# Two more pairs of blocks in layer one, with sums of weights made earlier and reloaded

## The chip, the cores and the metric

The kernel runs on one core of a Trainium2 chip. The metric is the device time of one execution in microseconds; lower is better. TensorE's matmul side is called PE and its weight loads PEld; DVE is VectorE, ACT is ScalarE, POOL is GpSimd and SP the sync engine, whose queue issues most DMAs.

## What is computed

A long convolution by FFT over 2 x 3008 tokens of 256 channels, and behind it two feed-forward layers of 256 to 2048 to 256. The weights come as 64-bit floats.

```python
X = np.fft.rfft(x, axis=1)
y = np.fft.irfft(X * F, n=x.shape[1], axis=1).astype(np.float32)   # F: filt_r + 1j * filt_i
x = y.reshape(6016, 256)
h = x @ moe_w_in                                  # layer one
g = np.where(h > 0.0, h, np.exp(np.minimum(h, 0.0)) - 1.0)
x = (g @ moe_w_out).astype(np.float32)
h = x @ moe2_w_in                                 # layer two
g = h * np.clip(h + 3.0, 0.0, 6.0) / 6.0
out = (g @ moe2_w_out).astype(np.float32)
```

## The kernel before

**Numbers and tiles.** Every operand of a matmul is held as a high part and a low part (fp32r), and a product is three matmuls (`mm3`, lines 83 to 86). The 6016 tokens are 12 blocks, ten of 512 columns and two (5 and 11) of 448. The 2048 hidden channels are 16 chunks f of 128. A first-layer product of one block and one f has two halves c, a second-layer product two halves d.

**Single blocks.** Layer one starts with blocks 0 to 2 side by side and goes on with the blocks of `SINGLES` one by one. A unit is one block and one f: 6 matmuls into the hidden channel (`g1`), ELU (ACT twice at lines 422 and 423, DVE at line 424), a split into high and low (`g_split`, ACT line 80 and DVE line 81), and 6 matmuls of the second product (`g2`), three units later. `NU` is the number of units, 160 here. The list `pre` holds what is issued ahead of each unit, its slot; a pair group has four slots.

**Pairs.** The other blocks are worked in pairs by Winograd's form of Strassen's scheme: a group is one pair and two f (q = 0 to 7), with seven block products (`prod`) where eight would be needed, and eight second products (`second`). The seven products need sums of the data blocks (`x_sums`, `x_part`, 4 and 7 operations for a pair) and sums of the weights (`w_sums`, three sums for two f). In the group, key (k, d) names one of four hidden tiles. `add` (line 543) joins two banks on DVE; for layer one and the keys (0, 0) and (0, 1) a min follows on DVE (line 546) and ACT does one exponential (line 559); the keys (1, 0) and (1, 1) take a Relu and an exponential on ACT (lines 556 and 557). `gate` (line 566 for layer one) and `low` (line 579) are DVE's, `high` (line 574) is ACT's. PE's order in a group of layer one is: products 1 and 2, second (0, 0) of the group before, products 6 and 5, second (1, 1), product 7, second (1, 0), half of second (0, 1), product 4, the other half, product 3 (`elu_group`). DVE's order from the end of a group is: `add` (0, 1) and its min, then in the next group `low` (1, 1), `add` (0, 0) with its min, `gate` (0, 1), `low` (1, 0), the first slot's jobs, `gate` (0, 0), `low` (0, 1), on which half of second (0, 1) waits.

**Filling.** Weights of layer two are taken apart from their 64-bit words on DVE and ACT while the units run (`w_words`, `w_parts`, and `w_sums`), and stored to DRAM (`scrw`, `scrs`), to be loaded from GpSimd's queue when layer one has released its tiles (`w_load`, `s_load`). `filling` lists these steps, 176 of them, and `count` says how many are issued in each slot. Layer one's own sums of weights are in there as well: chunks 0 to 2 early, in the tile that the FFT's `zt` had, chunks 3 to 7 at the very end of the filling, in tiles of the pool `p4` (21 tiles) that live until the pair round is over. The second batch's FFT runs in slots 48 to 96 beside the units: its filter products are DVE's lines 192 and 193, GpSimd's line 195, and splits on ACT and DVE (line 81) or GpSimd.

**Layer two** is six pairs, in the same form, with another gate.

Of the kernel before, what the change touches and what calls it, by code (L numbers as in the profile page):

```python
# [30 lines left out]
SINGLES = [3, 4, 5, 6, 11, 7, 8]  # L31
PAIRS = [[(9, 10)], [(0, 1), (2, 3), (4, 6), (7, 8), (9, 10), (5, 11)]]
# [15 lines left out]
def fft_conv_moe_moe2(ctx, tc, xp, fq, sg, cs1, cs1t, cs2, ci2, ci1, ident, w1i, w1o, w2i, w2o, out):  # L48
# [249 lines left out]

    def s_tile(layer, q):
        if q >= 3:  # L300
            sums[layer, q] = t4([P, 2, 4, P], F32R)
            return
        if q == 0:
            sums[layer] = p12.tile([P, 3, 2, 4, P], F32R, tag="zt", name=name("zt"))
        sums[layer, q] = sums[layer][:, q]

    def w_sums(layer, q):
# [24 lines left out]
        if layer:  # L332
            nc.sync.dma_start(scrs[q], _f32(r.rearrange("p q i f -> p (q i f)")))
        yield

# [129 lines left out]
    def x_sums(l, p, i):  # L465
# [7 lines left out]
        eng = nc.vector if (l, p) in ROUNDS[:2] else nc.gpsimd  # L473
# [55 lines left out]
    class Group:  # L529
# [10 lines left out]
        def add(self, key, u, bank_):  # L540
# [3 lines left out]
            if not self.l and key[0] == 0:  # L544
# [3 lines left out]
        def relu(self, key):  # L548
# [6 lines left out]
            elif key[0] == 1:  # L555
# [233 lines left out]
    def filling():  # L789
        yield from sums_run(range(3))  # L790
        yield from conv2
        yield from sums_run(range(3, GROUPS))
# [4 lines left out]
    count = {52: 2, 53: 1, 54: 2, 55: 1, 56: 2, 57: 1, 58: 1, 59: 2}  # L797
    count.update({85: 2, 86: 4, 87: 2, 88: 1, 89: 2, 90: 1, 91: 5, 92: 3, 93: 3})
    count.update({NU + n: 1 for n in range(5, 17, 2)})
    left = n_fill - sum(count.values())  # L800
    other = {n: 1 for n in (94, 95, 99, 108, 109, 115, 124, 125, 131, 140, 141, 147, 158)}
    other.update({n: other.get(n, 0) + 1 for n in (134, 138, 139, 142, 143, 146, 147, 150, 154, 155)})
    room = {n: 7 if 112 <= n < 128 else 8 for n in range(94, NU)}
    total, had, jobs = sum(room.values()), 0, left + sum(other.values())
    for n in range(94, NU):
        had += room[n]
        want = -(-jobs * had // total) - sum(other.get(m, 0) for m in range(94, n + 1))
        count[n] = max(0, want - sum(count[m] for m in range(94, n)))
    assert sum(count.values()) == n_fill
    for n, k in sorted(count.items()):  # L810
        at(pre, n, steps, fill, k)
    for q in range(GROUPS):
        at(pre, NU + max(4 * q + 5, 14), s_load, q)
    for f in range(NF):
        at(pre, NU + 4 * (f // 2) + 8, w_load, f)
# [5 lines left out]
    }  # L821
    for i, (l, p) in enumerate(ROUNDS):
        for q, jobs in AHEAD.items():
            for j, (fn, arg) in enumerate(jobs):
                lag = 2 + j if i == 0 else 0 if i == 1 and fn is x_part else 2
                at(pre, NU + 4 * (GROUPS * (i - 1) + q) + lag, fn, l, p, arg)
# [253 lines left out]
```

## Time and profile before

| | |
|---|---|
| median of 3 runs | 1105.84 us (1105.46 to 1106.04) |
| profiled execution, its own time | 1105.2 us |
| its span, first to last instruction | 1103.4 us |
| matmuls (PE) | 5046 |
| busy share PE, PEld, DVE, ACT, POOL | 99%, 83%, 84%, 73%, 11% |
| granted clock of TensorE | full speed (1.0) |

The page gives busy time by engine and for 40 slices of the span; a timeline lists instructions by start; windows give each engine's busy time in a stretch; waits say which instruction waited for which. In this execution unit 48 is at about 196 us and unit 94 at 357 us, the pair round of layer one (blocks 9 and 10) runs from about 532 to 614 us, and layer two from there on.

### The profile page before, as it was taken

What the parts mean: (1) busy time and instruction counts of PE and PEld (TensorE: products, weight loads), DVE (VectorE), ACT (ScalarE), POOL (GpSimd) and SP (SyncE); (2) the same over time, 40 slices, a digit from 0 to 9 for tenths busy, and PEclk for the clock granted to TensorE, in tenths of its full rate; (3) what the DMA queues carried; (4) which work ended last, traced back from release to release, by engine and by line L of the source; (5) the groups of instructions that cost most, each with busy time, mean ns of one, the idle gap of its engine ahead of it and who ended that gap; (6) DMA issues with size and microseconds to landing.
All of it is one profiled execution on the core that took longest, in us unless ns stands there. A gap on an engine that the chain in (4) does not pass through costs nothing.

```text
span 1103.4 us, 14295 instructions
## 1 busy us (share of the span) xinstructions
PE 1095.1 (99%) x5046; PEld 912.8 (83%) x5046; DVE 925.7 (84%) x1495; ACT 801.2 (73%) x1426; POOL 116.9 (11%) x109
## 2 busy tenths in 40 slices
PE   9999999999999999999999999999999999999998
PEld 6688888788799889888888888888888888888997
DVE  5889998789988999999898877778777787777766
ACT  3587777887677787887788777667667767766665
POOL 4500000035520000000011110010010010000000
PEclk9999999999999999999999999999999999999999
DMA  9991100455544434323155400100100100100100
GB/s 298 292 315 56 29 1 1 142 179 180 167 120 144 148 117 154 112 77 134 39 172 176 168 20 20 39 20 20 39 20 20 39 18 17 39 1 1 39 1 34
DMA packets 55784, 99.44 MB, mean 90 GB/s; under 512 B 4768, under 2 KB 33440, under 8 KB 55712
## 3 DMA queue, kind: packets, MB, share of 16 engines
q1 hardware_dynamic: 51424, 85.59, 23.6%
q0 software_dynamic: 3456, 12.58, 3.6%
q8 instruction: 39, 0.64, 0.2%
q10 hardware_dynamic: 832, 0.36, 0.1%
q14 instruction: 33, 0.27, 0.1%
HBM read 64.18 MB, written 34.34 MB: 89 GB/s over the span
## 4 chain that ended last, share of the span: by engine, by line
PE 90%; DVE 4%; DMA 2%; issue 1%; ACT 1%; POOL 1%; SPq 0%; POOLq 0%; ACTq 0%; DVEq 0%
PE ps L84 29%; PE ps L85 28%; PE ps L86 28%; PE ps L219 1%; PE ps L139 1%; DMA scr<-t 1%; DVE t L81 1%; DMA t<-in_xp 1%; POOL t L195 1%; DMA t<-scr 1%; PE ps L183 1%; PE ps L152 0%; PE ps L200 0%; DVE t L192 0%; PE ps L892 0%
## 5 line engine op out<-in xcount | busy, mean ns | idle before, releaser
L84 PE MATMUL ps<-t,w 128*128 128x512 f32 (+1 forms) x1256 | 486.7, 387 | 1.5 <-DVE t L81 1.1
L85 PE MATMUL ps<-t,w 128*128 128x512 f32 (+1 forms) x1256 | 484.2, 386 | 0.0
L86 PE MATMUL ps<-t,w 128*128 128x512 f32 (+1 forms) x1256 | 484.2, 385 | 0.0
L84 PEld LDWEIGHTS ps<-t,w 128*128 128x128 f32 x1256 | 236.1, 188 | 48.9 <-DVE t L579 1.5
L86 PEld LDWEIGHTS ps<-t,w 128*128 128x128 f32 x1256 | 235.9, 188 | 44.1
L85 PEld LDWEIGHTS ps<-t,w 128*128 128x128 f32 x1256 | 236.1, 188 | 42.9
L81 DVE TENSOR_TENSOR t<-t,t 128x512 fp32r<-128x512 f32 (+2 forms) x257 | 190.3, 748 | 3.0 <-ACT t L80 1.7
L80 ACT ACTIVATE t<-t 128x512 fp32r<-128x512 f32 (+2 forms) x269 | 160.4, 610 | 21.3 <-POOL t L195 17.8
L579 DVE TENSOR_TENSOR t<-t,t 128x512 fp32r<-128x512 f32 (+1 forms) x224 | 154.1, 706 | 22.2 <-ACT t L574 20.9
L537 ACT ACTIVATE t<-ps 128x512 f32<-128x512 f32 (+1 forms) x168 | 99.0, 589 | 87.1 <-PE ps L86 85.9
L422 ACT ACTIVATE t<-ps 128x512 f32<-128x512 f32 (+1 forms) x160 | 93.3, 583 | 69.8 <-PE ps L86 69.2
L574 ACT ACTIVATE t<-t 128x512 fp32r<-128x512 f32 (+1 forms) x224 | 134.3, 617 | 4.9 <-DVE t L564 4.7
L543 DVE TENSOR_TENSOR t<-ps,t 128x512 f32<-128x512 f32 (+1 forms) x168 | 113.3, 677 | 26.3 <-ACT t L537 21.6
L424 DVE SCALAR_TENSOR_TENSOR t<-t,ps 128x512 f32<-128x512 f32 (+1 forms) x160 | 107.0, 669 | 28.8 <-ACT t L423 25.9
L564 DVE SCALAR_TENSOR_TENSOR t<-t,t 128x512 f32<-128x512 f32 (+1 forms) x144 | 98.7, 712 | 33.7 <-ACT t L554 33.4
L554 ACT ACTIVATE t<-t,three 128x512 f32<-128x512 f32 (+1 forms) x144 | 97.4, 709 | 35.4 <-DVE t L543 34.7
L423 ACT ACTIVATE t<-t 128x512 f32<-128x512 f32 (+1 forms) x160 | 99.5, 622 | 5.1
L564 DVE SCALAR_TENSOR_TENSOR t<-t,ps 128x512 f32<-128x512 f32 (+1 forms) x48 | 32.6, 678 | 29.0 <-ACT t L554 29.0
L86 PE MATMUL ps<-t,t 128*128 128x512 f32 (+1 forms) x140 | 54.1, 386 | 0.0
L84 PE MATMUL ps<-t,t 128*128 128x512 f32 (+1 forms) x140 | 54.0, 386 | 0.0
L85 PE MATMUL ps<-t,t 128*128 128x512 f32 (+1 forms) x140 | 54.0, 386 | 0.0
L554 ACT ACTIVATE t<-ps,three 128x512 f32<-128x512 f32 (+1 forms) x48 | 32.6, 680 | 28.9 <-PE ps L86 28.9
(99 smaller groups left out, 998.5 us busy)
## 6 DMA issues: line engine op xcount, KB each, us to landing
t<-in_fq SPq DMA_DIRECT2D x24, 512.0 KB, 6.4
scrw<-t SPq DMA_DIRECT2D x16, 512.0 KB, 2.8
w<-scrw POOLq DMA_DIRECT2D x16, 512.0 KB, 4.0
t<-in_xp SPq DMA_DIRECT2D x16, 384.0 KB, 6.0
scr<-t SPq DMA_DIRECT2D x24, 256.0 KB, 2.8
t<-scr SPq DMA_DIRECT2D x16, 384.0 KB, 4.9
scrx<-t SPq DMA_DIRECT2D x10, 512.0 KB, 3.3
t<-scrx SPq DMA_DIRECT2D x10, 512.0 KB, 3.4
```

Of the source, the lines that this page charges most:

```text
L80: nc.scalar.activation(hi, src, AF.Copy)
L81: eng.tensor_tensor(out=lo, in0=src, in1=_f32(hi), op=ALU.subtract)
L84: nc.tensor.matmul(acc, wh, xl, start=start, stop=False, skip_group_check=more)
L85: nc.tensor.matmul(acc, wl, xh, start=False, stop=False, skip_group_check=more)
L86: nc.tensor.matmul(acc, wh, xh, start=False, stop=stop, skip_group_check=more)
L423: nc.scalar.activation(r[:, :n], r[:, :n], AF.Exp, scale=-1.0)
L424: nc.vector.scalar_tensor_tensor(out=r[:, :n], in0=r[:, :n], scalar=-1.0, in1=acc[:, :n], op0=ALU.add, op1=ALU.max)
L543: nc.vector.tensor_tensor(out=self.h[key][:, :n], in0=bank_[:, :n], in1=u[:, :n], op=ALU.add)
L554: nc.scalar.activation(r[:, :n], h, AF.Relu, bias=three)
L564: stt(out=r, in0=r, scalar=6.0, in1=h, op0=ALU.min, op1=ALU.mult)
L574: nc.scalar.activation(gh[:, : self.n], g[:, : self.n], AF.Copy)
L579: nc.vector.tensor_tensor(out=gl[:, :n], in0=g[:, :n], in1=_f32(gh[:, :n]), op=ALU.subtract)
```

## The change

Blocks 7 and 8 leave the singles and become a second pair of layer one, ahead of 9 and 10. `NU` is 128 then, the two pair rounds of layer one take 64 slots, and layer two begins at slot `L2` = 192 as before. Eight groups of 45 matmuls take the place of 32 units of 12.

All of layer one's sums of weights are made first in the filling (26 steps in slots 45 to 61, 6 in 85 and 86), then the weights of layer two, which now run on through both pair rounds and 14 slots of layer two. The sums 3 to 7 are stored to DRAM (`scr0`) and loaded again in each pair round, one group ahead of their use, from GpSimd's queue. The loads of layer two's sums from chunk 3 on, and of its last two weight chunks, come later. In a group of layer one only key (0, 1) keeps its min on DVE; (0, 0) takes the Relu on ACT. The operand sums of the first round of layer two are DVE's (`ROUNDS[:3]`). `LATER` says where the operands of the next pair are made during a pair round of layer one.

```diff
-SINGLES = [3, 4, 5, 6, 11, 7, 8]
-PAIRS = [[(9, 10)], [(0, 1), (2, 3), (4, 6), (7, 8), (9, 10), (5, 11)]]
+SINGLES = [3, 4, 5, 6, 11]
+PAIRS = [[(7, 8), (9, 10)], [(0, 1), (2, 3), (4, 6), (7, 8), (9, 10), (5, 11)]]
...
+    scr0 = {q: dram.tile([P, 1024], F32, name=f"scr0_{q}") for q in range(3, NF // 2)}
...
-        if layer:
-            nc.sync.dma_start(scrs[q], _f32(r.rearrange("p q i f -> p (q i f)")))
+        if layer or q >= 3:
+            nc.sync.dma_start(scrs[q] if layer else scr0[q], _f32(r.rearrange("p q i f -> p (q i f)")))
...
+    def s0_load(q):
+        s_tile(0, q)
+        nc.gpsimd.dma_start(sums[0, q].rearrange("p q i f -> p (q i f)"), scr0[q])
...
-        eng = nc.vector if (l, p) in ROUNDS[:2] else nc.gpsimd
+        eng = nc.vector if (l, p) in ROUNDS[:3] else nc.gpsimd
...
-            if not self.l and key[0] == 0:
+            if not self.l and key == (0, 1):
                 self.g[key] = t2([P, 512])
                 nc.vector.tensor_scalar_min(self.g[key][:, :n], self.h[key][:, :n], 0.0)
...
-            elif key[0] == 1:
+            elif key != (0, 1):
                 nc.scalar.activation(r[:, :n], h, AF.Relu, scale=-1.0)
                 nc.scalar.activation(r[:, :n], r[:, :n], AF.Exp, scale=-1.0)
...
-        yield from sums_run(range(3))
+        yield from sums_run(range(GROUPS))
         yield from conv2
-        yield from sums_run(range(3, GROUPS))
+        yield from sums_run([])
...
-    count = {52: 2, 53: 1, 54: 2, 55: 1, 56: 2, 57: 1, 58: 1, 59: 2}
+    count = {n: 1 for n in range(45, 52)}
+    count.update({n: 2 for n in range(52, 62)})
+    count[58] = 1
+    L2 = NU + 4 * GROUPS * len(PAIRS[0])
...
-    count.update({NU + n: 1 for n in range(5, 17, 2)})
...
-        want = -(-jobs * had // total) - sum(other.get(m, 0) for m in range(94, n + 1))
+        want = -(-236 * had // 800) - sum(other.get(m, 0) for m in range(94, n + 1))
         count[n] = max(0, want - sum(count[m] for m in range(94, n)))
+    left, late = n_fill - sum(count.values()), L2 + 14 - NU
+    for n in range(late):
+        count[NU + n] = left * (n + 1) // late - left * n // late
...
-        at(pre, NU + max(4 * q + 5, 14), s_load, q)
+        at(pre, L2 - 4 * GROUPS + 14 if q < 3 else L2 + 4 * q - 4, s_load, q)
+        if q >= 3:
+            for r in range(len(PAIRS[0])):
+                at(pre, NU + 4 * (GROUPS * r + q - 1), s0_load, q)
     for f in range(NF):
-        at(pre, NU + 4 * (f // 2) + 8, w_load, f)
+        at(pre, max(L2 - 4 * GROUPS + 4 * (f // 2) + 8, L2 + 16 if f > 13 else 0), w_load, f)
...
+    LATER = {
+        2: [(x2_load, 0, 2), (x2_load, 1, 2)], 3: [(x_sums, 0, 2)], 4: [(x_sums, 1, 2), (x_part, 1, 0)],
+        5: [(x_sums, 2, 2), (x_part, 2, 0)], 6: [(x_sums, 3, 2), (x_part, 6, 0)],
+        7: [(x_part, 5, 0), (x_part, 7, 0)], 8: [(x_part, 4, 0), (x_part, 3, 1)],
+    }
```

## Rows read from the trace of the kernel before

**Rows 1.** the first part of the page: busy time, share of the span, instructions:

```profile
PE 1095.1 (99%) x5046; PEld 912.8 (83%) x5046; DVE 925.7 (84%) x1495; ACT 801.2 (73%) x1426; POOL 116.9 (11%) x109
```

**Rows 2.** timeline of PE in layer two: start, duration (us), engine, line, instruction:

```profile
749.94 0.39 PE L84 MATMUL ps<-t,w 128*128 128x512 f32 x1
...
759.46 0.39 PE L84 MATMUL ps<-t,w 128*128 128x512 f32 x1
```

**Rows 3.** windows: length; busy time of PE, PEld, DVE, ACT, POOL:

```profile
480.00:490.00 10.00, 10.00 (x46) 8.27 (x45) 9.93 (x19) 7.61 (x15) 0.00 (x0) 1.00 0.13 52
...
570.00:580.00 10.00, 10.00 (x46) 8.26 (x45) 9.77 (x17) 8.31 (x15) 1.42 (x3) 1.00 0.51 157
```

**Rows 4.** timeline of DVE among the single blocks:

```profile
481.00 1.28 DVE L81 TENSOR_TENSOR t<-t,t 128x512 fp32r<-128x512 f32 x2
...
482.21 0.68 DVE L284 TENSOR_TENSOR t<-t,t 128x512 f32<-128x512 f32 x1
...
487.33 0.75 DVE L323 TENSOR_TENSOR t<-t,t 128x256 f32<-128x256 f32 x2
```

**Rows 5.** timeline of DVE in the pair round, groups 2 and 3:

```profile
552.74 0.68 DVE L543 TENSOR_TENSOR t<-ps,t 128x512 f32<-128x512 f32 x1
...
557.87 0.68 DVE L579 TENSOR_TENSOR t<-t,t 128x512 fp32r<-128x512 f32 x1
...
562.92 0.69 DVE L543 TENSOR_TENSOR t<-ps,t 128x512 f32<-128x512 f32 x1
...
563.64 0.43 DVE L546 TENSOR_SCALAR t<-t 128x512 f32<-128x512 f32 x1
...
563.99 0.68 DVE L579 TENSOR_TENSOR t<-t,t 128x512 fp32r<-128x512 f32 x1
```

**Rows 6.** timeline of PE in group 2 of the pair round:

```profile
550.77 0.39 PE L84 MATMUL ps<-t,w 128*128 128x512 f32 x1
...
558.60 0.50 PE L84 MATMUL ps<-t,w 128*128 128x512 f32 x1
...
558.94 0.39 PE L85 MATMUL ps<-t,w 128*128 128x512 f32 x1
```

**Rows 7.** waits from 520 to 640 us: total, number, longest:

```profile
DVE t L566 <- ACT t L557: 6.6, 14, 0.9
...
PEld ps L84 <- DVE t L579: 1.1, 3, 0.6
...
PEld ps L84 <- ACT t L537: 0.5, 2, 0.4
```

**Rows 8.** timeline of DVE in slots 59 and 60, with idle time before:

```profile
233.93 1.42 DVE L329 TENSOR_TENSOR t<-t,zt 128x512 f32<-128x512 f32 x1 [0.27 <-ACT zt L327]
...
239.29 0.69 DVE L424 SCALAR_TENSOR_TENSOR t<-t,ps 128x512 f32<-128x512 f32 x1 [0.69 <-ACT t L423]
```

**Rows 9.** timeline of POOL (GpSimd): its additions of line 195:

```profile
277.27 1.28 POOL L195 TENSOR_TENSOR t<-t,t 128x512 f32<-128x512 f32 x1 [1.11 <-DVE t L193]
...
284.01 1.29 POOL L195 TENSOR_TENSOR t<-t,t 128x512 f32<-128x512 f32 x1 [1.10 <-issue]
...
292.34 1.30 POOL L195 TENSOR_TENSOR t<-t,t 128x512 f32<-128x512 f32 x1 [2.82 <-DVE t L193]
...
300.71 1.29 POOL L195 TENSOR_TENSOR t<-t,t 128x512 f32<-128x512 f32 x1 [2.84 <-DVE t L193]
```

**Rows 10.** timeline of PE at its stop near 302 us:

```profile
301.78 0.39 PE L86 MATMUL ps<-t,w 128*128 128x512 f32 x1
...
302.60 0.50 PE L84 MATMUL ps<-t,w 128*128 128x512 f32 x1 [0.44 <-DVE t L81]
```

**Rows 11.** DMA: landing of line 338's loads, then two issue groups (KB each, median):

```profile
DMA to landing us min/median/max: 4.6/5.1/7.4
...
scrs<-t SPq DMA_DIRECT2D x8, 512.0 KB, 3.0
...
t<-scr SPq DMA_DIRECT2D x12, 256.0 KB, 3.5
```

More of the change, by code (lines that the diff above doesn't have):

```diff
@@ L796, in fft_conv_moe_moe2 @@
     n_fill = 7 * NF + 8 * GROUPS
-    count = {52: 2, 53: 1, 54: 2, 55: 1, 56: 2, 57: 1, 58: 1, 59: 2}
+    L2 = NU + 4 * GROUPS * len(PAIRS[0])
+    count = {n: 1 for n in range(45, 52)}
+    count.update({n: 2 for n in range(52, 62)})
+    count[58] = 1
     count.update({85: 2, 86: 4, 87: 2, 88: 1, 89: 2, 90: 1, 91: 5, 92: 3, 93: 3})
-    count.update({NU + n: 1 for n in range(5, 17, 2)})
-    left = n_fill - sum(count.values())
-    other = {n: 1 for n in (94, 95, 99, 108, 109, 115, 124, 125, 131, 140, 141, 147, 158)}
-    other.update({n: other.get(n, 0) + 1 for n in (134, 138, 139, 142, 143, 146, 147, 150, 154, 155)})
+    other = {n: 1 for n in (94, 95, 99, 108, 109, 115, 126, 102, 106, 107, 110, 111, 114, 118, 122, 123)}
+    other[115] = 2
+    for n in range(94, NU):
+        count[n] = 0
     room = {n: 7 if 112 <= n < 128 else 8 for n in range(94, NU)}
-    total, had, jobs = sum(room.values()), 0, left + sum(other.values())
+    had = 0
     for n in range(94, NU):
         had += room[n]
-        want = -(-jobs * had // total) - sum(other.get(m, 0) for m in range(94, n + 1))
+        want = -(-236 * had // 800) - sum(other.get(m, 0) for m in range(94, n + 1))
         count[n] = max(0, want - sum(count[m] for m in range(94, n)))
+    left, late = n_fill - sum(count.values()), L2 + 14 - NU
+    for n in range(late):
+        count[NU + n] = left * (n + 1) // late - left * n // late
     assert sum(count.values()) == n_fill
@@ L821, in fft_conv_moe_moe2 @@
     }
-    for i, (l, p) in enumerate(ROUNDS):
+    LATER = {
[3 more added lines that the diff above has]
+    }
+    for i, (l, p) in enumerate(ROUNDS):
+        start = NU + 4 * GROUPS * (i - 1)
+        if 0 < i <= len(PAIRS[0]):
+            for q, jobs in LATER.items():
+                for fn, arg, lag in jobs:
+                    at(pre, start + 4 * q + lag, fn, l, p, arg)
+            continue
         for q, jobs in AHEAD.items():
             for j, (fn, arg) in enumerate(jobs):
-                lag = 2 + j if i == 0 else 0 if i == 1 and fn is x_part else 2
-                at(pre, NU + 4 * (GROUPS * (i - 1) + q) + lag, fn, l, p, arg)
+                at(pre, start + 4 * q + 2 + (0 if i else j), fn, l, p, arg)
     parts = {}
```

## The prediction, made before the changed kernel was built or run

> **What bounds the kernel now.** I read the first part of the page first: PE is busy for 1095.1 us, 99% of the span [rows 1]. The reader should then look at PE's timeline in a quiet stretch: from 749.94 to 759.46 us 42 matmuls of 512 columns start, one every 0.2267 us, with nothing between [rows 2]. The kernel is bound by the number of its matmuls. The windows show what stands behind: DVE is busy 9.93 of 10 us among the single blocks and 9.77 in the pair round of layer one, ACT 7.61 and 8.31 [rows 3]. So PE is the bound and DVE is second by a hair, just where the change puts work. On DVE the cost of an operation is the distance between starts, since neighbours overlap by 0.08: two of 512 columns hold it for 1.21 us (482.21 less 481.00), 0.605 each, though one lasts 0.68; two of 256 columns last 0.75 together, so 0.67 or 0.335 each [rows 4].
>
> **What goes.** Four units of single blocks (two blocks, two f) hold 48 matmuls; a pair group does the same with 21 for the products and 24 for the second layer, 45. Eight groups save 24, and 24 x 0.2267 = 5.44 us, all of it on PE and so on the path. The Trainium skill, TensorE: Matmul & The Clock Gate, section Back-to-back issue gap, gives about 131 ns per matmul of 512 columns in a sustained stream with weight loads; by that the gain would be 24 x 0.131 = 3.1 us (an estimate from that page). No trace here agrees: [rows 2] show 227 ns for such a stream, and the measurement decides.
>
> **What comes, on DVE.** A pair group costs DVE more than four single units: 3 adds, 4 gates, 4 lows at about 0.605 and a min, against 4 gates and 4 subtractions. The pair round of today shows the add with its min at 0.72 + 0.35 (starts at 562.92, 563.64, 563.99) [rows 5]. One of two mins goes to ACT as a Relu, so a group is 11 x 0.605 + 0.11 + 0.34 = 7.1 us, against 8 x 0.605 = 4.8 for four units. PE needs 45 x 0.2267 = 10.20 us for a group. The rest is added from the schedule: the filling has 176 steps; by the counts 26 now run in slots 45 to 61 (11 before), 23 in 85 to 93, 59 in 94 to 127, 68 in the 78 slots after, 55 of them in the two pair rounds. Taken step by step these cost 1.3 to 2.5 us per group; each round also makes the next round's operands (4 sums, 7 splits, 6.6 us) and copies out. Over groups 1 to 15 the need is 148.3 us, 9.89 per group of 10.20, or 97%. Before, the singles ran at 9.93 of 10 with PE busy throughout [rows 3], so a mean of 97% alone costs nothing; what costs is the order within the groups.
>
> **The pair rounds.** Take group 2 of today: it starts on PE at 550.77; its add of (0,1) starts at 552.74, the subtraction that PE waits for at 557.87, and PE's 34th matmul starts at 558.60 instead of 550.77 + 33 x 0.2267 = 558.25 [rows 5, 6], 0.35 late. From the add to the end of that subtraction is 557.87 + 0.68 - 552.74 = 5.81, with one split of 0.6 in it; without the second min it is 4.75 plus what stands in the group's first slot. So PE waits when the add's start, plus 4.75, plus the first slot, passes 7.43 us. Carrying DVE's backlog from group to group (10.20 a group to spend, the gates of the group's end not before 0.77 into the next): groups 4 and 6 need 10.5 and 10.7, group 7 begins its add at 1.35 with 1.54 in the first slot: 0.21 us late. Group 8, at the seam of the rounds, needs 12.0 with two output copies; group 9 starts its add at 3.0 and loses 0.7 and 0.3. Group 15 has two splits and a step (1.8) in its first slot: 0.6 late. Group 1 loses 0.35 in two stops, as today, where the output copies of the last single come in between. Each of these six stops (two in groups 1 and 9) costs 0.11 more, for the matmul after it starts 0.34 later, not 0.23 [rows 6]. Sum: 2.8 us. Today's pair round has 1.6 us of weight-load waits on DVE and ACT, the longest 0.6 [rows 7]; that one is the stop above, and it cost PE 0.35 + 0.11 = 0.46, so all of them are worth 1.2, and go. Net +1.6 us, between -1 (no stop at all) and +4 (0.15 a group more than I count). ACT's extra Relu (16 x 0.54) is hidden: ACT is busy 8.31 of 10 there [rows 3], and its gate comes out before DVE reaches it.
>
> **The earlier sums.** Slots 60 and 61 gain the adds of chunk 6 and the close of chunk 5, 4 x 0.335 + 2 x 0.605 = 2.55 us of DVE, at about 238 us. There GpSimd works too, and a DVE subtraction that meets it takes 1.42 instead of 0.68 [rows 8]; I take half of one such stretch, 2.9 in all. DVE's one idle time there is 0.69 [rows 8], so it falls 2.2 us behind. Behind it on DVE stand the filter products, and behind those GpSimd's additions (L195) and ACT's splits. Does it catch up? L195 comes at 277.27 and 284.01, 6.74 us apart [rows 9], against PE's 30 x 0.2267 = 6.80 for two units and their filter products: hardly, 0.06 a turn. Then today's DVE loses more: 292.34 and 300.71 come 8.33 and 8.37 after the one before, 1.6 late each [rows 9], 3.2 together, and PE stops behind a DVE subtraction, 0.82 instead of 0.23 at 302.60 [rows 10], 0.7 with the slow restart. So PE bears about 2.4 us of lag, which is used up today; of the 2.2 new us some 1.9 remain by then and go to PE. +1.9 us, between 0 (the slack is larger than this one stop shows) and 2.5. The new stores of the five chunks sit on SP ahead of the z loads and wait for DVE's last step; a z load has four slots, two such turns or 13 us, and such loads land in 3.5 [rows 11], so a lag of 2 is covered.
>
> **At nothing.** Singles 94 to 127 hold 76 jobs against 79 before. Ten reloads on GpSimd's queue are issued a group ahead: 10.2 + 12 x 0.2267 = 12.9 us before their first product, and such chunks landed 4.6 to 7.4 us after issue in this same stretch [rows 11]. The layer-two weight loads are on that queue as well; each waits for PE to finish a group that is over by then. If the cover went, a chunk that lands at 14 would cost 1.1 us, ten of them 11. The layer-two sums from chunk 3 on are now loaded one group ahead too, between GpSimd's operand sums, additions as L195 is, of 1.3 us [rows 9]: 12.9 - 7.4 - 1.3 leaves 4. Buffers: more tiles of both pools are alive in the pair rounds, so an ACT or DVE instruction may wait for the store that last read its buffer; no row shows it, a store lands in 3.0 us [rows 11]; I take 0, since a store ends long before its buffer's turn comes again in a pool of some 20, and keep 0 to 3.0 for the range.
>
> **Sum.** The profiled run took 1105.2 us (span 1103.4, 1.8 around it). -5.4 + 1.6 + 1.9 = -1.9. The median of the runs is 1105.84, 0.64 above the profiled one: 1105.84 - 1.9 = 1103.9 us.
>
> **Rivals.** (a) The covers hold: the lag near 240 us is absorbed and the pair rounds lose no more than today: 1105.84 - 5.4 = 1100.4. For it: singles and pair groups at 9.93 and 9.77 of DVE with PE busy throughout [rows 3]. Against it: PE's stops behind DVE at 558.60 and 302.60 [rows 6, 10].
> (b) Slower: DVE becomes the pace of the 16 pair groups. Today DVE idles 6.6 us in 14 waits before its gates [rows 7], some 0.8 a group, where it had room. If those waits stay and the added work cannot fill them, a group takes 9.89 + 0.8 = 10.7, and 16 x 0.5 = 8 us are lost: 1105.84 - 5.4 + 1.9 + 8 - 1.2 = 1109.1. It decides from 0.31 a group on; slower than before by 0.2% from about 0.74. Against it: in the loaded groups of today DVE is already busy 9.77 of 10 [rows 3], so the waits do shrink where the queue is full. The Trainium skill, Perfetto Trace Analysis, section Identifying the Most-Contended Engine, takes the engine of highest occupancy and judges TensorE by its weight loads; here that is DVE (9.77 of 10 against 8.26), and by that rule more DVE work for less PE work lengthens the stretch. In that window PE was busy for 10.00 of 10 [rows 3], so the trace bears it out only in part.
> (c) A reload or a reused buffer is late a few times: 1 to 3 us on top, 1105 to 1107.
>
> **How the numbers follow.** A difference of 0.2% (2.2 us) is about what a measurement can tell from none. Forecast 0.48, of which a quarter (0.12) falls below 1103.6 and 0.36 within; its own range is 1102 to 1106. (a) 0.32, faster. (b) 0.12, slower. (c) 0.08, within. So faster 0.44, same 0.44, slower 0.12. The range leaves out (b) and the lowest part of (a): 1100.2 to 1106.8.
>
> **What would show it.** Right: 24 matmuls fewer; PE still at 0.227; DVE over 95% through both pair rounds; weight loads waiting on DVE's low at the seam and at the rounds' ends, and more stop at 290 to 305 us than the 0.7 of today. Wrong: no PE waits in either place (a); matmul starts spread out evenly through the rounds (b); waits on a GpSimd load (c).

## The result, and the profile after

The changed kernel takes 1111.78 us, median of 4 runs (1111.63 to 1112.39), against 1105.89 us for the kernel before in the same job: a ratio of 1.0055, 95% interval 1.0038 to 1.0072. It is slower by 5.9 us, outside the range (1100.2 to 1106.8). The profiled run took 1111.63 us, its span (first to last instruction) is 1109.9 us, 6.4 us more than before.

The first part of the page of the kernel after, and its chain of work by engine (what the last instruction waited for, followed back to the start); then the chain of the kernel before:

```profile
PE 1096.3 (99%) x5022; PEld 906.5 (82%) x5022; DVE 940.8 (85%) x1526; ACT 811.8 (73%) x1453; POOL 125.6 (11%) x119
...
PE 76%; DVE 14%; ACT 4%; issue 3%; DMA 2%; POOL 1%; SPq 0%; DVEq 0%; POOLq 0%; ACTq 0%
```

```profile
PE 90%; DVE 4%; DMA 2%; issue 1%; ACT 1%; POOL 1%; SPq 0%; POOLq 0%; ACTq 0%; DVEq 0%
```

The 24 matmuls are gone (5022 for 5046, [rows 1]). PE still shows 99%, since a matmul is recorded with 0.39 us though one starts every 0.2267 us: the busy share of PE doesn't show short stops. The chain does: PE falls from 90% of it to 76%, and DVE rises from 4% to 14%.

To find the place I read off the timelines when the Relu of the same unit of single blocks starts (L422 before, L428 after; units count from 0), and the first matmul of layer two:

| stretch | before | after | difference |
|---|---|---|---|
| start to unit 48 | 196.20 | 196.56 | +0.36 |
| unit 48 to unit 94 (transform of the second batch) | 160.79 | 163.75 | +2.96 |
| unit 94 to unit 127 (single blocks) | 86.74 | 86.74 | 0.00 |
| unit 127 to layer two (singles and one pair before, two pairs after) | 168.81 | 170.05 | +1.24 |
| layer two to the end | 490.89 | 492.76 | +1.87 |

In the fourth line 5.44 us of matmuls are saved, so 6.7 us were lost there. Two places lose: the transform, and the pair groups with the first groups of layer two (1.7 us of the last line). The first line is the start of the run, which differs between runs of equal code (last section).

**The transform.** Waits of the weight loads from 200 to 310 us in the kernel after, and DVE's timeline at slots 60 and 61 (start, duration, engine, line, instruction), first of the kernel after, then of the kernel before:

```profile
PEld ps L84 <- DVE t L81: 5.4, 11, 0.9
```

```profile
239.13 0.41 DVE L325 TENSOR_TENSOR t<-w 128x256 f32<-128x256 f32 x1
...
240.59 0.68 DVE L430 SCALAR_TENSOR_TENSOR t<-t,ps 128x512 f32<-128x512 f32 x1
241.19 1.38 DVE L81 TENSOR_TENSOR t<-t,t 128x512 fp32r<-128x512 f32 x1
242.49 0.68 DVE L331 TENSOR_TENSOR t<-t,t 128x512 f32<-128x512 f32 x1
...
243.93 1.39 DVE L192 TENSOR_TENSOR t<-ps,t 64x512 f32<-64x512 f32 x2
```

```profile
239.89 0.69 DVE L81 TENSOR_TENSOR t<-t,t 128x512 fp32r<-128x512 f32 x1
240.61 1.39 DVE L192 TENSOR_TENSOR t<-ps,t 64x512 f32<-64x512 f32 x2
```

Before, the same wait is 1.6 us in 4, and the filter products of L192 start at 240.61. They now start 3.32 later, 2.96 of it not from the start of the run. Exactly these 2.96 us are missing at unit 94. The sums (L325) took the 0.69 us in which DVE was idle [rows 8], the split behind them overlapped an instruction of GpSimd (240.73 to 242.02) and took 1.38 us, where the split at 239.89 took 0.69 before, and the close of chunk 5 (L331, L333) follows.

**The pair groups.** The window from the start of group 1 to layer two (length; busy time and instructions of PE, PEld, DVE, ACT, POOL; granted clock, DMA share, GB/s), and the waits in it (us in total, number, longest):

```profile
456.36:617.10 160.74, 157.24 (x677) 125.37 (x676) 150.45 (x264) 134.86 (x243) 12.51 (x24) 1.00 0.41 137
```

```profile
ACT t L562 <- DVE t L549: 14.8, 15, 1.8
DVE t L572 <- ACT t L563: 9.1, 17, 1.5
PEld ps L84 <- DVE t L585: 7.0, 13, 1.0
ACT t L565 <- DVE t L552: 4.8, 14, 0.5
...
DVE t L549 <- ACT t L543: 0.4, 1, 0.4
```

Fifteen groups of 45 matmuls need 153.0 us; they took 160.74, 10.72 a group instead of 10.20. DVE worked 150.45 us and waited 9.5 for ACT, which is the whole stretch but 0.8. ACT meanwhile waits 14.8 for DVE's adds and 4.8 for its mins: the two hand work to and fro. Group 5 shows a stop of PE (ACT, DVE, then PE; in brackets the idle time before an instruction and what ended it):

```profile
501.08 0.63 ACT L565 ACTIVATE t<-t 128x512 f32<-128x512 f32 x1 [0.43 <-DVE t L552]
501.62 0.61 ACT L282 ACTIVATE t<-t 128x512 fp32r<-128x512 f32 x1
502.13 0.66 ACT L261 ACTIVATE t<-raw 128x512 f32<-128x512 f32 x1
502.70 0.62 ACT L80 ACTIVATE t<-t 128x512 fp32r<-128x512 f32 x1
...
504.35 0.63 ACT L563 ACTIVATE t<-t 128x512 f32<-128x512 f32 x1
```

```profile
505.02 0.69 DVE L572 SCALAR_TENSOR_TENSOR t<-t,t 128x512 f32<-128x512 f32 x1 [0.64 <-ACT t L563]
505.63 0.69 DVE L585 TENSOR_TENSOR t<-t,t 128x512 fp32r<-128x512 f32 x1
```

```profile
505.81 0.40 PE L86 MATMUL ps<-t,w 128*128 128x512 f32 x1
506.37 0.50 PE L84 MATMUL ps<-t,w 128*128 128x512 f32 x1 [0.16 <-DVE t L585]
506.71 0.40 PE L85 MATMUL ps<-t,w 128*128 128x512 f32 x1
```

ACT's Exp of key (0,1) (L565) waits for DVE's min; behind it stand two jobs of the filling (L282, L261) and a split (L80), and only then the u2 copy (ACT's copy of product 6, L543) and the Relu (L562) and Exp (L563) of (0,0). DVE, which is late, must wait 0.64 us for that Exp, since its gate is next in its own order; the subtraction that PE needs (505.63) stands behind the gate. PE loses 0.33 us at 506.37, and 0.11 more with the matmul after it, which starts 0.34 later and not 0.23.

That wait is the only one of its kind. By DVE's timeline the 9.1 us behind L563 are 0.6 in this one at gate (0,0), 2.7 in 8 at gate (1,1) and 5.8 in 8 at gate (1,0), at the end of a group. The longest, at the end of group 7 (ACT, then DVE):

```profile
529.36 0.63 ACT L562 ACTIVATE t<-t 128x512 f32<-128x512 f32 x1 [1.18 <-DVE t L549]
...
530.56 0.62 ACT L282 ACTIVATE t<-t 128x512 fp32r<-128x512 f32 x1
531.08 0.66 ACT L261 ACTIVATE t<-raw 128x512 f32<-128x512 f32 x1
...
532.25 0.63 ACT L563 ACTIVATE t<-t 128x512 f32<-128x512 f32 x1
```

```profile
532.92 0.69 DVE L572 SCALAR_TENSOR_TENSOR t<-t,ps 128x512 f32<-128x512 f32 x1 [1.53 <-ACT t L563]
```

ACT waits for DVE's add, makes Relu and Exp of (1,1), two jobs of the filling, and then Relu and Exp of (1,0), for which DVE waits. Six groups have a filling job of ACT in this place, and their waits are 4.9 of the 5.8 us.

### The profile page after: what moved, and what is told of

Read it like the earlier page. It is cut to its first block, busy times and chain, and to the rows that moved or that the text cites. A ratio compares the mean times of both kernels' runs of the same rounds, so it can differ in the third digit from the quotient of the medians.

```text
span 1109.9 us, 14358 instructions
## 1 busy us (share of the span) xinstructions
PE 1096.3 (99%) x5022; PEld 906.5 (82%) x5022; DVE 940.8 (85%) x1526; ACT 811.8 (73%) x1453; POOL 125.6 (11%) x119
## 4 chain that ended last, share of the span: by engine, by line
PE 76%; DVE 14%; ACT 4%; issue 3%; DMA 2%; POOL 1%; SPq 0%; DVEq 0%; POOLq 0%; ACTq 0%
PE ps L84 24%; PE ps L86 24%; PE ps L85 24%; DVE t L585 3%; DVE t L549 2%; DVE t L572 2%; DVE t L81 2%; PE ps L219 2%; PE ps L139 1%; DMA raw<-in_w1i 1%; ACT t L562 1%; ACT t L563 1%; DMA t<-scr 1%; POOL t L195 1%; DVE t L192 1%
## 5 line engine op out<-in xcount | busy, mean ns | idle before, releaser
L84 PE MATMUL ps<-t,w 128*128 128x512 f32 (+1 forms) x1216 | 472.2, 388 | 4.5 <-DVE t L585 2.4
L85 PE MATMUL ps<-t,w 128*128 128x512 f32 (+1 forms) x1216 | 468.4, 385 | 0.0
L86 PE MATMUL ps<-t,w 128*128 128x512 f32 (+1 forms) x1216 | 468.3, 385 | 0.0
L84 PEld LDWEIGHTS ps<-t,w 128*128 128x128 f32 x1216 | 228.3, 188 | 55.1 <-DVE t L585 7.5
L86 PEld LDWEIGHTS ps<-t,w 128*128 128x128 f32 x1216 | 228.3, 188 | 43.1
L85 PEld LDWEIGHTS ps<-t,w 128*128 128x128 f32 x1216 | 228.4, 188 | 41.3
L585 DVE TENSOR_TENSOR t<-t,t 128x512 fp32r<-128x512 f32 (+1 forms) x256 | 176.3, 703 | 21.4 <-ACT t L580 20.1
L81 DVE TENSOR_TENSOR t<-t,t 128x512 fp32r<-128x512 f32 (+2 forms) x228 | 171.4, 759 | 2.7 <-ACT t L80 1.5
L543 ACT ACTIVATE t<-ps 128x512 f32<-128x512 f32 (+1 forms) x192 | 112.7, 587 | 77.0 <-PE ps L86 75.5
L80 ACT ACTIVATE t<-t 128x512 fp32r<-128x512 f32 (+2 forms) x240 | 142.7, 609 | 28.3 <-POOL t L195 25.0
L580 ACT ACTIVATE t<-t 128x512 fp32r<-128x512 f32 (+1 forms) x256 | 154.2, 617 | 8.2 <-DVE t L570 6.7
L428 ACT ACTIVATE t<-ps 128x512 f32<-128x512 f32 (+1 forms) x128 | 74.0, 578 | 49.1 <-PE ps L86 48.7
L430 DVE SCALAR_TENSOR_TENSOR t<-t,ps 128x512 f32<-128x512 f32 (+1 forms) x128 | 85.3, 666 | 20.7 <-ACT t L429 19.6
L429 ACT ACTIVATE t<-t 128x512 f32<-128x512 f32 (+1 forms) x128 | 79.3, 619 | 4.1
L84 PE MATMUL ps<-t,t 128*128 128x512 f32 (+1 forms) x160 | 62.0, 388 | 0.0
L86 PE MATMUL ps<-t,t 128*128 128x512 f32 (+1 forms) x160 | 61.8, 386 | 0.0
L85 PE MATMUL ps<-t,t 128*128 128x512 f32 (+1 forms) x160 | 61.8, 386 | 0.0
L480 POOL TENSOR_TENSOR t<-t,t 128x512 f32<-128x512 f32 (+1 forms) x15 | 23.7, 1579 | 292.0 <-DVE t L549 249.9
L570 DVE SCALAR_TENSOR_TENSOR t<-t,ps 128x512 f32<-128x512 f32 (+1 forms) x48 | 32.5, 677 | 26.7 <-ACT t L560 26.6
```

Source lines behind the costliest of these rows:

```text
L80: nc.scalar.activation(hi, src, AF.Copy)
L81: eng.tensor_tensor(out=lo, in0=src, in1=_f32(hi), op=ALU.subtract)
L84: nc.tensor.matmul(acc, wh, xl, start=start, stop=False, skip_group_check=more)
L85: nc.tensor.matmul(acc, wl, xh, start=False, stop=False, skip_group_check=more)
L86: nc.tensor.matmul(acc, wh, xh, start=False, stop=stop, skip_group_check=more)
L430: nc.vector.scalar_tensor_tensor(out=r[:, :n], in0=r[:, :n], scalar=-1.0, in1=acc[:, :n], op0=ALU.add, op1=ALU.max)
```

## The experiments

Theories. **U**: a pair group costs DVE its work plus its waits for ACT, whatever the order. **W**: DVE's amount of work alone decides. **Q, V**: the order of the jobs makes the waits and the stops, in Q that of ACT's jobs, in V that of the dependent steps on both engines. **L**: the transform's loss is the lag from slots 60 and 61. **M**: it comes from the added steps in slots 45 to 59. In the table "groups 1 to 15" is their time (in the windows below) less 675 x 0.2267 = 153.0, "layer two" the same for its first four groups, "transform" units 48 to 94. The kernel before had medians of 1105.9 to 1106.7 beside these runs, so medians that differ by less than 1 us are compared by the stretches.

| kernel | median | groups 1 to 15 | layer two | transform |
|---|---|---|---|---|
| after | 1111.78 | 7.7 | 1.7 | 163.75 |
| one min more on DVE | 1117.66 | 13.3 | 1.8 | 163.75 |
| both mins on ACT | 1110.93 | 6.3 | 1.8 | 163.73 |
| no ACT jobs of the filling | 1108.05 | 3.3 | 1.7 | 163.80 |
| no DVE jobs of the filling | 1104.00 | 1.1 | 0.0 | 163.74 |
| filling in slots 1 and 2 | 1118.54 | 10.6 | 4.9 | 163.73 |
| low (0,1) first, ahead of the copy | 1116.52 | 11.6 | 2.2 | 163.71 |
| low (0,1) first, behind the copy | 1112.83 | 8.2 | 2.4 | 163.77 |
| four steps to slots 45 to 48 | 1111.18 | 7.7 | 1.8 | 162.65 |
| four steps to 36, 38, 40, 42 | 1110.28 | 7.8 | 1.7 | 160.82 |
| low (0,1) first, behind the copy; four steps to 24, 28, 32, 36 | 1110.73 | 8.2 | 2.3 | 160.78 |
| the same with both mins on ACT | 1108.66 | 6.6 | 2.0 | 160.78 |
| nine steps early | 1108.40 | 5.6 | 2.1 | 161.20 |
| one pair | 1108.96 | 0.2 (7 groups) | 0.0 | 163.76 |

**One min more on DVE.** The min that the change gives to ACT's Relu goes back:

```
-            if not self.l and key == (0, 1):
+            if not self.l and key[0] == 0:
-            elif key != (0, 1):
+            elif key[0] == 1:
```

> The kernel after, with the negative part of key (0,0) taken by VectorE's min again instead of ScalarE's Relu: in each of the 16 pair groups ScalarE has one operation less (0.54 us by the row of a Relu) and VectorE one more (0.34 to 0.46 us). Theory Q (ScalarE's order: the pair groups stop because the gates of the first half come late out of ScalarE's queue, and the extra Relu is one of the jobs that stand ahead of them): gate (0,0) and (0,1) come out 0.5 us earlier, some half of the 7.1 us of stops between 450 and 622 us goes, 1107.5 to 1110. Theory W (VectorE has too much work there, whatever the order): 16 x 0.34 to 0.46 us more on the engine that is late, 1113 to 1118. Had the added Relu been hidden, as the prediction says, only VectorE's part would be seen, as in theory W.

1117.66 us, 5.9 above the kernel after, as W had it. Windows of groups 1 to 15, and waits there:

```profile
456.90:623.22 166.32, 159.36 (x677) 124.50 (x676) 156.70 (x279) 128.42 (x228) 12.39 (x24) 1.00 0.40 133
```

```profile
PEld ps L84 <- DVE t L585: 13.7, 21, 1.5
DVE t L572 <- ACT t L563: 8.5, 16, 1.5
```

DVE works 6.25 us more, waits 1.0 less (8.5 for 9.5), and the groups take 5.6 us more: work put on DVE goes to the end nearly one for one. Q falls in this form: with one job less on ACT's queue the groups got slower. The Relu on ACT was worth its place.

**Both mins on ACT.** The same step the other way:

```
-            if not self.l and key == (0, 1):
-                self.g[key] = t2([P, 512])
-                nc.vector.tensor_scalar_min(...)
-            elif key != (0, 1):
+            else:
```

> The kernel after, with the last min of VectorE in the pair groups of layer one (key (0,1)) made by ScalarE's Relu as well: the step of the change taken once more. Theory W (VectorE is the pace of the pair groups: its work plus its waits; moving a min to it cost 5.9 us): 16 x 0.34 us less, as long as there are stops to remove: 1106 to 1107. Theory Q (the order of ScalarE's jobs makes the gates late; its Relu of 0.54 us replaces a min on the same path, 0.1 to 0.2 us longer): 1111 to 1114.

1110.93 us: 0.85 less (1.4 in the groups) where W alone gives 5.

```profile
456.82:616.12 159.30, 156.78 (x677) 125.52 (x675) 145.47 (x248) 141.72 (x257) 12.57 (x24) 1.00 0.42 139
```

```profile
DVE t L567 <- ACT t L560: 13.1, 33, 1.5
```

DVE works 5.0 us less and waits 4.2 more. W alone falls too: most of what this second min took off DVE came back as waits for ACT, 3.4 us of them at gate (0,1), where there were none. The first min, moved by the change itself, paid 5.6 of 6.25 us.

**No ACT jobs of the filling, no DVE jobs of the filling.** In the pair groups of layer one, the first has memsets on GpSimd in the place of the filling's three ACT operations (one of them shown), the second leaves out the filling's DVE operations behind the absolute value and those of the sums (not shown):

```
-        nc.scalar.activation(hl[:, 0, :], v, AF.Copy)
+        if lean[0]: nc.gpsimd.memset(_f32(hl[:, 0, :]), 1.0)
+        else: nc.scalar.activation(hl[:, 0, :], v, AF.Copy)
```

> The kernel after, but in the pair groups of layer one the added work of the other batch and of the sums leaves out its ScalarE operations (the absolute value, the copies into the high halves and of the sums of x are memsets on GpSimd, so this part of the computation is left out); VectorE's part of the added work stays whole. Theory Q (ScalarE's order): nothing stands ahead of the copy, Relu and Exp any more, most of the 7.1 us of stops between 450 and 622 us and part of the 1.6 us behind it goes: 1104 to 1107. Theory W (VectorE's amount of work): VectorE has all its work still, 1110.5 to 1112.

> The kernel after, but in the pair groups of layer one the added work leaves out its VectorE operations (the low halves and the sums of weights are not computed, so this part of the computation is left out); its ScalarE operations stay where they are in the order. Theory Q (ScalarE's order): ScalarE's copy, Relu and Exp come as late as before, and VectorE only waits longer for them; most stops stay, 1108.5 to 1111.5. Theory W (VectorE's amount of work): with some 3 us of work per group less VectorE is never behind, 7 us of stops go, 1104 to 1106.

1108.05 and 1104.00 us. Windows and DVE's waits, the first, then the second:

```profile
456.69:613.05 156.36, 155.08 (x677) 125.99 (x675) 150.52 (x264) 128.74 (x228) 20.62 (x39) 1.00 0.45 148
```

```profile
DVE t L582 <- ACT t L573: 5.0, 13, 0.8
```

```profile
456.93:611.09 154.16, 153.63 (x677) 126.41 (x676) 126.86 (x209) 135.92 (x243) 15.38 (x30) 1.00 0.43 142
```

```profile
DVE t L595 <- ACT t L586: 23.6, 39, 1.5
DVE t L572 <- ACT t L566: 3.0, 8, 0.8
```

Without the ACT jobs DVE works as long as it did (150.52), waits 4.5 us less, and the groups take 4.4 less. The waits at gate (1,0) fall from 5.8 to 1.5, those at (1,1) stay at 2.7: nearly all of the gain is in the place shown above. Without the DVE jobs DVE has 26.6 us of waits, which cost nothing: PE is the bound again, and 1.1 us remain, as in the pair round before. So the filling makes the loss, by both engines: its DVE part as work, its ACT part as waits. The sum of DVE's work and waits by itself doesn't name the pace: it fills 153.5 of 154.2 us here too, where 26.6 of it are free. What names it is that less filling on either engine makes the groups shorter.

**The order.** First the filling's steps in slots 1 and 2 of a group alone, with the splits of the next round's operands in slot 1 (changed in `LATER`, not shown). Slots 2 and 3 stand between the two Relus of the place shown above:

```
-        count[NU + n] = left * (n + 1) // late - left * n // late
+        m = NU + 4 * (n // 4) + (1 if n % 4 < 2 else 2)
+        count[m] = count.get(m, 0) + left * (n + 1) // late - left * n // late
```

> The kernel after, with the same work in another order: in the pair groups the steps of the added work stand in slots 1 and 2 of each group alone, and the splits of the operands in slot 1, so that nothing of it stands ahead of the copy, Relu and Exp of the first half or of key (1,0). The amount of work is the same on each engine. Theory Q (order): VectorE's waits for ScalarE before its gates (10.8 us in 17 waits between 450 and 615 us) fall to about 7 us, as where the ScalarE jobs were left out (7.4 us, 1108.05 us), and the time to 1106.5 to 1109. Theory W in its pure form (amount of work alone): 1111 to 1113.

1118.54 us, 6.8 more, which neither theory had. The stops leave the second product of (0,1) and come at the products whose bank ACT's copies set free: weight loads wait 9.5 us for the copy of L543 (2.7 in the kernel after). Then the two steps of group 5 in the other order, high and low of (0,1) ahead of the Exp and gate of (0,0), once ahead of the u2 copy and once behind it:

```
+        if old: old.high((0, 1))      # first run: here; second run: behind the next line
         u2 = g.copy(a)
         g.relu((0, 0))
-        if old: old.high((0, 1))
-        g.gate((0, 0))
         if old: old.low((0, 1))
+        g.gate((0, 0))
```

> The kernel after, with two operations of each pair group of layer one in another order: the copy of the high half of key (0,1) stands ahead of the u2 copy on ScalarE, and the subtraction of its low half ahead of gate (0,0) on VectorE. The work is the same; VectorE has 0.6 us to do while ScalarE makes the Relu and Exp of (0,0), and the operands of the second products at which TensorE stops come 1 to 1.5 us earlier. Theory V (a group costs VectorE its work plus its waits for ScalarE, 9.9 + 0.7, and the waits come from the order of the dependent steps on both engines): VectorE's waits before its gates fall from 10.8 to 5 us or less between 450 and 615 us, and the time by 3.5 to 6 us, to 1106 to 1108.3. Theory W (amount of work alone): the stops move to another place, 1110.5 to 1112.

> The reordering of the pair groups once more, with the copy of the high half of key (0,1) behind the u2 copy and ahead of the Relu of (0,0), not ahead of the u2 copy. In the run before it product 7 stopped instead, because the u2 copy, which sets its bank free, stood behind the high half. Theory V (the stops come from the order of the dependent steps: low (0,1) is made behind a gate that waits for two ScalarE operations): the stops at the second product of (0,1) go (ten of them, 0.1 to 0.8 us and the slow restart), none comes at product 7, 1105.5 to 1108. Theory U (a group costs VectorE its work plus waits whatever the order, some 10.6 us): stops move elsewhere again, 1110.5 to 1113.

1116.52 and 1112.83 us. Waits of the first, window and waits of the second, and PE in its group 5:

```profile
PEld ps L84 <- ACT t L543: 13.9, 21, 1.1
DVE t L572 <- ACT t L563: 12.6, 23, 1.5
```

```profile
456.36:617.55 161.19, 158.25 (x677) 124.77 (x675) 150.36 (x263) 135.12 (x242) 12.38 (x24) 1.00 0.41 137
```

```profile
DVE t L572 <- ACT t L563: 9.3, 18, 1.5
...
PEld ps L84 <- ACT t L543: 6.4, 10, 1.2
...
PEld ps L84 <- DVE t L585: 4.1, 13, 0.7
```

```profile
504.42 0.50 PE L84 MATMUL ps<-t,t 128*128 128x512 f32 x1 [0.40 <-ACT t L543]
```

The stop at 506.37 is gone in the second run, and one at product 7 (504.42) stands in its place. The waits for the low halves fall from 7.0 to 4.1, those for the copies rise from 2.7 to 6.4; the sum of DVE's work and waits is the same, and so is the time of the groups within 0.5 us. The first has 3.6 us more waits of DVE (13.1 for 9.5) and 3.8 more time; it lay above both expectations. So V falls for these orders: none lost less than the 7.7 us of the kernel after. U's "whatever the order" is too much as well, for two of the three orders cost 2.9 and 3.8 us more. And neither of the last two touches the place where DVE waits most: there are 5.8 us at gate (1,0) and 2.7 at (1,1) in both, as in the two runs with a min moved. An order that keeps ACT's filling out of it, in slots 0 and 1 alone, was not tried, so that no order helps isn't shown.

**The transform.** The four steps of slots 60 and 61 elsewhere:

```
+    count.update({45: 2, 46: 2, 47: 2, 48: 2, 60: 0, 61: 0})            # first run
+    count.update({36: 1, 38: 1, 40: 1, 42: 1, 60: 0, 61: 0})            # second run
+    count.update({24: 1, 28: 1, 32: 1, 36: 1, 60: 0, 61: 0})            # third run, with the order of the last kernel above
```

> The kernel after, with the four steps of slots 60 and 61 (sums of weights beside the transform of the second batch) put into slots 45 to 48 instead. It tests the 2.96 us that the stretch from unit 48 to unit 94 became longer. Theory L (VectorE, once behind at slots 60 and 61, does not catch up and stops TensorE turn after turn): with those slots as they were, the stretch takes 160.8 to 161.5 us again, with 0 to 0.8 us lost at slots 45 to 48 instead, 1108.5 to 1110. Theory M (the stops there come from the steps in slots 45 to 59, which are also new or two for one): they stay or grow, 1111 to 1113.

> The kernel after, with the four steps of slots 60 and 61 in slots 36, 38, 40 and 42, where VectorE is idle for 0.7 to 0.9 of 10 us. Theory L (the 2.9 us between units 48 and 94 are the lag from slots 60 and 61, and the 1.7 us stop near 198 us of the last such run came from two steps a slot in 45 to 48): the stretch takes 160.8 to 161.2 us, 1108.5 to 1109.2. If the lag comes of the sums made beside single blocks wherever they stand: 1111 to 1112.

> The same, with the four steps of slots 60 and 61 in slots 24, 28, 32 and 36: 2.9 us less than the reordering alone, since the stretch between units 48 and 94 takes 160.8 us again. Theory V: 1102.5 to 1105. Theory U: 1107.5 to 1110.

1111.18, 1110.28 and 1110.73 us. The new stop of the first run, that of the second, and the weight loads' wait from 200 to 310 us in the third:

```profile
200.38 0.50 PE L84 MATMUL ps<-t,w 128*128 128x512 f32 x1 [1.46 <-DVE t L430]
```

```profile
180.31 0.50 PE L85 MATMUL ps<-t,w 128*128 128x512 f32 x1 [0.70 <-DVE w L286]
```

```profile
PEld ps L84 <- DVE t L81: 1.6, 4, 0.9
```

The first time lies in M's range: 162.65 remain in this stretch, but 1.7 us of it are the stop at 200.38 behind the crowded slots, so this run leaves L and M open. The second has 160.82 and loses 1.0 near slot 42, hence its time above the 1108.5 to 1109.2 of L; the third has 160.78, as the kernel before, and loses nothing earlier (units 0 to 48 take 128.31, before 128.29). Its profile is 2.8 us below the run without the early steps, its median 2.1. L holds, and M falls, for slots 45 to 59 are as full in the last two: the loss of 2.96 us is that of four steps in slots 60 and 61.

**One pair.** Blocks 7 and 8 stay single; the earlier sums, the reloads and the Relu are kept, and the doses of the filling follow from the longer singles (210 for 236 in `want`):

```
-SINGLES = [3, 4, 5, 6, 11]
+SINGLES = [3, 4, 5, 6, 11, 7, 8]
-PAIRS = [[(7, 8), (9, 10)], ...
+PAIRS = [[(9, 10)], ...
```

> The kernel after with one pair only: blocks 7 and 8 stay single, the earlier sums, the reloads and the Relu stay. It parts the two halves of the change. Theory V (the stops come from the added work in the pair groups, which with two pairs has to stand there): with 32 more slots of single blocks for it the stops between the last single block and layer two fall to 1 to 2 us, the 2.7 us of saved matmuls of the second pair are given back, the 2.9 us near 240 to 305 us stay: 1108 to 1110. If the earlier sums or the reloads made the stops of the pair groups: 1111 to 1114.

1108.96 us (its job's kernel before: 1106.15). The expectation took half of the saved matmuls; the pair holds all 24, 5.44 us. The earlier sums, the reloads and the Relu together cost 2.8 us, which is the transform's loss, and nothing in the pair round:

```profile
543.90:615.55 71.65, 71.65 (x317) 58.99 (x315) 61.01 (x102) 60.98 (x108) 11.01 (x21) 1.00 0.56 188
```

There DVE works 8.7 us a group, not 10.0, since 32 more slots of singles carry the filling. The second pair then saves 5.44 us and loses 7.5 more in groups 1 to 15 and 1.7 in layer two, 3.8 in sum; the two spans (1109.9 and 1106.6) are 3.3 apart. The reloads have no part in it: in the waits of PE, DVE and ACT in the kernel after from 450 to 660 us none is for a load. The runs of the kernel before went from 1105.24 to 1115.07 in this job, so the reading rests on the stretches and not on the ratio (1.0006, 0.998 to 1.003).

**Less work for the pair groups.** Nine steps in slots 12 to 36, none in 60 and 61, so that five fewer are left for the pairs:

```
+    count.update({n: 1 for n in (12, 15, 18, 21, 24, 27, 30, 33, 36)})
+    count.update({60: 0, 61: 0})
-    at(pre, 82, w_raw, 1, 0)
+    at(pre, 46, w_raw, 1, 0)
```

> The kernel after, with the amount of VectorE's work in the pair groups made smaller and nothing else: nine steps of the added work stand in every third slot from 12 to 36, none in 60 and 61, and the first weight load of layer two is issued at slot 46, so that five steps fewer are left for the pair groups. Theory U (a group costs VectorE its work plus waits, whatever the order): 2.9 us less between units 48 and 94, and 5 x 0.62 = 3.1 us less in the pair groups: 1105 to 1107. Theory V (order): only the 2.9 us, 1108.5 to 1109.5.

```profile
454.18:612.81 158.63, 156.69 (x676) 125.33 (x675) 148.14 (x258) 134.53 (x241) 12.43 (x24) 1.00 0.40 132
```

1108.40 us: the transform gains 2.5, the pair groups 2.1 of the 3.1 expected (DVE's work falls by 2.3), and layer two loses 0.3 more. The sign is U's; the size follows what the steps really held of DVE.

**Combinations**, for a kernel below both. The filling in the middle with both mins on ACT and early steps; the first order above with early steps, and with both mins; the second order with early steps and both mins, then with nine and with fourteen steps early:

> The three edits together: both mins on ScalarE, the steps of the added work in the middle of the pair groups, the four steps in slots 36 to 42. If VectorE's work plus its waits is the pace of the pair groups, and the lag that of slots 60 and 61, both go and what is left are stops at the seam and behind it of 1 to 2 us: 1100.5 to 1103. If the edits take the same stops away they don't add up: 1103 to 1106.

> The same reordering, and the four steps of slots 60 and 61 in slots 24, 28, 32 and 36 (one in four slots instead of one in two, so that the stop of 0.86 us near 179 us does not arise). The stretch between units 48 and 94 takes 160.8 us again, none is lost before: 2.9 us less than the reordering alone. Theory V: 1103 to 1105.5, below the kernel before. Theory W: 1107.5 to 1109.

> The last one with the min of key (0,1) on ScalarE as well. By itself this step was worth 0.85 us, since ScalarE's longer chain gave most of it back in waits (10.8 to 14.8 us). If the reordering takes ScalarE off that chain, it is worth up to 16 x 0.34 us where stops remain: 1 to 3 us below the run without it. If ScalarE is the pace by now: 0 to 2 us above it.

> The last one with the min of key (0,1) on ScalarE too: 16 x 0.34 us less on VectorE, 16 x 0.54 us more on ScalarE. If stops are left that VectorE's amount of work makes: 1 to 3 us below the run without it; if ScalarE's order makes them, 0 to 2 us above it.

> The same nine steps early, on top of the reordering and of both mins on ScalarE (1108.66 us as it was). Theory U: 5 x 0.62 = 3.1 us less, 1104.8 to 1106.5. If ScalarE is the pace there by now: 1107.5 to 1109.

> The same with fourteen steps early, in every second slot from 10 to 36: ten fewer for the pair groups, 6.2 us. Theory U: 1102 to 1104 if VectorE's idle time in the first transform (0.3 to 1.1 of 10 us) takes all of them, 1104 to 1107 if PE stops there for part of it.

1118.28, 1113.95, 1112.26, 1108.66, 1110.46 and 1110.35 us. None is below the kernel before, and only the two steps to both mins (1.7 and 2.1 us less) came as expected. Both mins on ACT are worth 2.1 us once (0,1) comes first (1110.73 to 1108.66), more than the 0.85 alone, so order and amount act together. Fourteen steps don't fit into the first transform: units 0 to 48 take 131.49 instead of 128.31. And the pair groups didn't gain by them: against the run with four early steps DVE works 4.3 us less there (141.3 for 145.7) and waits 3.7 more (17.3 for 13.6), and the groups lose as much (6.7 and 6.6). Why is open. The run with nine steps meets a new wait, in DVE's timeline at 575 us:

```profile
575.02 0.69 DVE L480 TENSOR_TENSOR t<-t,t 128x512 f32<-128x512 f32 x1 [3.50 <-DMA t<-scrx]
```

It waits for the load of a block for the next round while the DMA engines are busy for 94% of 560 to 580 us (81% after, and no such wait). It started 2.5 us later besides and scatters over 4.3 us; what its five steps are worth there stays open.

## Why the prediction was wrong

**The saved matmuls**: right, 24 x 0.2267 = 5.44 us.

**The pair rounds**: the step that failed. It carried DVE's backlog from group to group by DVE's work alone, 148.3 us for groups 1 to 15 against 153, and counted six stops, 2.8 us in all, +1.6 net; 7.7 us were lost, +6.7 net. The work was nearly right: 150.45 us. What it put at nothing are the waits for ACT. It saw them (6.6 us in 14 waits, [rows 7]), and took them for slack that shrinks when the queue is full. They shrank, but not enough. The seven groups of the kernel before, and DVE's waits there:

```profile
540.08:612.54 72.46, 72.32 (x316) 58.76 (x315) 64.64 (x112) 58.23 (x104) 10.97 (x21) 1.00 0.50 163
```

```profile
DVE t L566 <- ACT t L557: 6.0, 13, 0.9
DVE t L543 <- ACT t L537: 0.8, 2, 0.4
```

There DVE worked 9.23 us a group and waited 0.97. In the kernel after it worked 10.03 and waited 0.63, and the two together are more than PE's 10.20. The stops came at nine of the fifteen groups, not at four. In each of the nine one stands at the 34th matmul, the place that the prediction had named, and these cost 4.8 of the 7.7 us by PE's timeline: the place was right, the number and size were not. An engine that is behind can still wait, when the engine that it waits for has itself waited for it and has other jobs in between, as at the end of group 7; ACT's waits for DVE's adds and mins rose from 1.0 us a group (6.7 in seven) to 1.3 (19.6 in fifteen).

That is rival (b), which was given 0.12: it said 9.89 + 0.8 = 10.7 a group, and 10.72 came. The closeness is in part luck, for the work was 0.14 higher and the waits 0.17 lower than it had them, and its sign, starts spread out evenly, did not come: some groups lost nothing, others up to 1.3. Its argument against itself, that DVE at 9.77 of 10 has no waits left [rows 3], looked at one window of 10 us.

The rule that stood beside (b), in the Trainium skill, Perfetto Trace Analysis, section Identifying the Most-Contended Engine, takes the engine of highest occupancy and judges TensorE by its weight loads. By that it is DVE in the pair groups (150.45 of 160.74, against 125.37 for the loads), and here that gave the right sign. It doesn't show the other part, for DVE is at 94%, not full, and the waits for ACT fill the rest.

**ACT's extra Relu**: hidden, said the step. Giving the min back to DVE cost 5.9 us, so the move was right. Its reason, that this gate comes out before DVE reaches it, held but for the 0.6 us of group 5. But ACT's time is not free elsewhere, as the second move (0.85 us) and the run without ACT's filling (3.7 us less) show.

**The stops moved on into layer two**, where nothing was costed: the last steps of the filling stand beside its first groups, which lose 1.7 us. In the run without the filling's DVE part, of which little is left there too (6 operations for 16), it is 0.0.

**The earlier sums**: right in place and mechanism, too small in size: 2.96 us for 1.9, and above the bound of 2.5. Two terms: the lag was 2.96 and not 2.2, since the six operations held DVE for 2.90 (1.46 and 1.44 between starts) and not 2.55, the split that met GpSimd took 0.58 more where some 0.35 was allowed, and 0.24 of lag was there already before the first of them; and nothing of it was absorbed, where 0.3 of slack was assumed.

**At nothing**: singles 94 to 127 take 86.74 us in both, no weight load or product waits on a reload, and with one pair these parts together cost nothing beyond the transform. Rival (c) did not come, except in experiments (3.5 us at 575.02, and 0.7 for the same kind of load with nine steps early alone).

In sum -5.44 + 7.72 - 1.05 (what the seven groups of the pair round lost before) + 1.72 + 2.96 + 0.36 (a later start) = 6.3 of the 6.4 us between the two spans. One count of the prediction is off: slots 45 to 61 held 12 steps before, not 11; no term uses it. Not tried: the filling in uneven doses, and ACT's filling kept out of the place between the two Relus. Groups 2, 10, 11 and 12 lost nothing in the kernel after, most of those in which the next round's operands are made lost. Five fewer steps gave 2.1 us and not 3.1 since they took only 2.3 us of work off DVE.

## What to carry to other kernels

Where two engines that each work their instructions in order hand results to each other inside a loop, budget each of them by work plus the waits that it has for the other. Don't take those waits as slack that vanishes under load: here work grew by 0.8 us a group, and the waits shrank by 0.3. Find in which step of the loop the waits are before moving anything: 8.5 of the 9.1 us here stood at two gates. Moving a min, or the order around another gate, left them as they were; leaving out ACT's jobs ahead of the second took 4.3 us off them. Work moved from the fuller engine to the other paid 5.6 us for the first min and 1.4 for the second, and none of the three orders tried was better. Less work for the pair of them paid in the three runs that changed little else (2.1, 4.4 and 6.6 us in the groups), not in the combinations, so look for the slots of other stages that carry it at no cost, and measure again. And ask where a lag on an engine that runs at the pace of the bound can be caught up: here 2.96 us at 244 us arrived whole 116 us later.

## What was not expected of the hardware

A 512 KB load of layer two's weights landed 3.7 us after issue by the median of the page of the kernel after, 4.2 from 560 to 580 us there, where the DMA engines were busy for 81% of the time, and 9.7 in the same stretch of the run with nine steps early and the new order, where they were busy for 94%. And the start scatters: the first single block's Relu comes between 67.92 and 70.74 us among kernels whose code up to there is the same, so that differences of 1 us are better read from a stretch than from the whole.
